# A staircase of single, paired and four-wide row tiles for gate/up, new due times, and down pieces in three steps

## The chip, the cores and the metric

The kernel runs on one core of one Trainium2 chip. The metric is device time in microseconds (us). TensorE is called PE below, VectorE DVE, ScalarE ACT, GpSimd POOL and SyncE SP; PSUM is the memory of eight banks into which PE writes, and from which DVE and ACT copy ("evict") to SBUF.

## What is computed

With `x` of 2048 rows and 640 columns, the output is `x + A(xn) + B(xn)`, where `xn` is the layernorm of `x`:

```python
def _A_ref(x, w_r, w_i):
    X = rfft2(x, axes=(-2, -1)) * (w_r + 1j * w_i)
    return irfft2(X, s=(S, D), axes=(-2, -1))

def _B_ref(x, w_gate, w_up, w_down):
    g = einsum("bsd,df->bsf", x, w_gate)
    u = einsum("bsd,df->bsf", x, w_up)
    return einsum("bsf,fd->bsd", g * u, w_down)

xn = _layernorm(x)
return x + _A_ref(xn, A_w_r, A_w_i) + _B_ref(xn, B_w_gate, B_w_up, B_w_down)
```

The weights `w_gate` and `w_up` are 640 x 1536, `w_down` is 1536 x 640, and `w_r`, `w_i` are 2048 x 321.

## The kernel before, in words

The rows are cut into 16 row tiles of 128, the 1536 hidden features into 12 blocks of 128, called features 0 to 11, and the 640 columns into five blocks of 128.

**Order.** No engine's order is written by hand. Each piece of work is a task with engines it may run on, an estimated duration, a priority (a lower number goes first) and what it reads and writes. `_Sched.plan` (line 155) lists them in advance: for each engine it takes the best priority, lets another task go first if that one ends within a slack (1500 ns for PE, 100 for names in `urgent`, line 1265, tile transposes `T0_0` to `T0_3` among them), and hands out PSUM banks. `caps` (lines 564 to 567) bound how many bank holdings a class may have at once: `glu` 4 (gate/up of 512 columns), `glu2` 2 (narrower gate/up), `acc` 5 (down), `a` 2 (pairs of banks for transposes and transforms). Each engine then runs its list in order, with semaphore waits.

**Stages.** (1) Loads of `x` (tiles 0 to 3 one by one, then 4 and 8 tiles) and of gate/up weights (features in groups 2, 2, 2, 2, 4) go out on SP; 10 warm-up rounds and small fill matmuls (lines 738 and 749) occupy PE meanwhile. (2) Layernorm by tile (groups of `_LN_GROUPS`; line 762): statistics on DVE (L785, L794) or ACT (L767, L776), then subtract and scale (L824, L831 or L830). Tiles 0 to 3 are transposed on PE (`T0`, L849) and copied to `XT`; later tiles by a transposing DMA (L837). (3) Forward transform over 8 groups of two tiles: butterflies S1 to S5 on DVE (L891 to L925), then a transform `R` on PE (L938) and its copy to `U`. (4) Gate/up (below). (5) When all of `U` is there, the spectral stage for 16 steps: D (L1055), C (L1078), multiplication by the filter on DVE (L1093, L1096), inverse IA (L1129, L1130), copy to `Z2`. (6) Inverse transform I on PE (L1158), by two tiles inverse butterflies V1 to V5 on DVE (L1182 to L1215). (7) Down: for each tile and half of the columns (the last tile in three pieces) 12 matmuls over the features into one bank (`ACC`, L1236), one more for the inverse transform (`IV`, L1248), the final addition of `x` on DVE (`FIN`, L1256), and a store.

**Gate/up.** For a group of row tiles ("chunk") and a feature, five matmuls for gate and five for up stream the chunk's columns of `XT`. `_CHUNKS` (line 508) holds tiles 0 and 1 alone, tiles 2-3 as a pair, and three chunks of four tiles. Chunks under four tiles take L997: one unit is two features, gate and up side by side in one bank for each (2 x 128 or 2 x 256 columns). Chunks of four take L977: one unit is one feature, gate and up in a bank of 512 columns each. ACT or DVE copies each bank to SBUF (L718 on ACT, L719 on DVE, helpers with many users), and DVE multiplies the two copies into `HT` (L1013 for four tiles, L1014 else). The units are sorted by the later of two due times, that of the rows (`c_at`) and that of the weights (`w_at`), and numbered for their priority (40 and up):

```python
w_at = [6.0 + opts.get("w_rate", 2.2) * opts.get("w_step", (0, 1, 2, 3, 4, 4))[ft // 2] for ft in range(12)]
c_at = [6.3 + opts.get("c_rate", 2.6) * (b0 + nb - 1) for b0, nb in _CHUNKS]
units = sorted((max(c_at[ci], w_at[ft | 1]), ci, ft) for ci in range(len(_CHUNKS))
               for ft in range(0, 12, 1 if _CHUNKS[ci][1] == 4 else 2))
```

**Down pieces.** Those of tiles 0 to 2 are three tasks of 5, 4 and 3 features (`cuts`, line 1229), the other 27 pieces one task of 12. The region of `w_down` for features 0 to 6 is taken by inverse tables until the spectral stage is over.

Of the kernel before, what the change touches and what calls it, by code (L numbers as in the profile page):

```python
# [504 lines left out]
_NW = 3  # L505
_WQ = 4
_GW_LOADS = ((0, 2), (2, 2), (4, 2), (6, 2), (8, 4))
_CHUNKS = ((0,1),(1,1),(2,2),(4,4),(8,4),(12,4))
_LP = 321
_YS = 1090  # L510
_NY = 3
# [39 lines left out]
def _build(nc, A_x, A_w_r, A_w_i, B_w_gate, B_w_up, B_w_down, out, opts=None):  # L551
    opts = opts or {}
    tabs = _build_tables()
    es = contextlib.ExitStack()
    with es:
# [7 lines left out]
        sch = _Sched()  # L563
        sch.caps = {"glu": opts.get("cap_glu", 4), "acc": opts.get("cap_acc", 5), "fill": 1}
        sch.caps["b"] = opts.get("cap_b", 3)
        sch.caps["glu2"] = opts.get("cap_glu2", 2)
        sch.caps["a"] = opts.get("cap_a", 2)
        lay = {}
        cur = [0]

        def alloc(name, size, at=None):
            if at is None:
                off = cur[0]
                cur[0] += size
            else:
                off = at
            lay[name] = (off, size)
            return sch.buf(name, off, size)
# [9 lines left out]
        b_x = alloc("X", 16 * 640, at=lay["Z2"][0])  # L588
# [166 lines left out]

        for gi, (b0, nb) in enumerate(_X_LOADS):
            dma("ld_x%d" % gi, v_x[:, b0:b0 + nb, :], xv[:, b0:b0 + nb, :], 128 * nb * (1800 if nb == 4 else 1400 if nb == 1 else 1280),
                [(b_x, ("s", b0, b0 + nb))], prio=(0.0, 0.003, 0.02, 0.03, 0.042, 0.06)[gi])
        muls = {}
        sd0 = None  # L760
        aset = set(opts.get("act_set", (1,))) | set(range(opts.get("act_stats", 6), 16))
        for gi, (b0, nb) in enumerate(_LN_GROUPS):
            pbase = 1.0 + 0.05 * gi if gi < 4 else opts.get("ln_prio", 6.1) + 0.05 * (gi - opts.get("ln_lead", 4))
            for b in range(b0, b0 + nb):
                if b in aset:
                    def em_sm(c, b=b):
# [53 lines left out]
            for b in range(b0, b0 + nb):  # L820
# [21 lines left out]
                def em_t0(c, b=b):  # L842
                    bk = bank_of(c.t)
                    ins = None
                    for j in range(5):
# [7 lines left out]
                       prio=pb, bank="pair" if b < opts.get("e0_split", 2) else "single", cls="a")  # L853
# [28 lines left out]
        for g in range(8):  # L882
            b = 2 * g
            gr = g % 2
            pf = opts.get("f_prio", 5.8) + 0.05 * g

            def em_s1(c, b=b, gr=gr):
                ins = None
# [64 lines left out]
        for i, (f0, nf) in enumerate(_GW_LOADS):  # L953
            for w_ in range(2):
# [1 line left out]
                    gvs[w_][:, :, f0 * 128:(f0 + nf) * 128], 5 * 128 * nf * (340 if nf == 2 else 280),  # L956
                    [(b_gw, ("s", w_ * _NGW + f0, w_ * _NGW + f0 + nf))], prio=(0.004, 0.012, 0.022, 0.032, 0.05)[i] + 0.001 * w_,
                    q="act" if w_ and i < 1 else "sp")
        w_at = [6.0 + opts.get("w_rate", 2.2) * opts.get("w_step", (0, 1, 2, 3, 4, 4))[ft // 2] for ft in range(12)]
        c_at = [6.3 + opts.get("c_rate", 2.6) * (b0 + nb - 1) for b0, nb in _CHUNKS]  # L960
        units = sorted((max(c_at[ci], w_at[ft | 1]), ci, ft) for ci in range(len(_CHUNKS))
                       for ft in range(0, 12, 1 if _CHUNKS[ci][1] == 4 else 2))
        for ui, (at_, ci, ft0) in enumerate(units):
            b0, nb = _CHUNKS[ci]
            n = 128 * nb
            rows = slice(b0 * 128, b0 * 128 + n)
            rr = ui % 3
            pu = 40.0 + 0.005 * ui
            pe_ = opts.get("eg_prio", 5.0) + 0.001 * ui
            ph_ = opts.get("h_prio", 5.0) + 0.001 * ui  # L970
            for u in range(2):
                ft = ft0 + u
                if nb == 4:
                    def em_gu4(c, ft=ft0, w=u, rows=rows):
                        bk = bank_of(c.t)
                        for j in range(5):
                            ins = c.e.matmul(ps[:, bk, :], v_gw[:, w, j, ft, :], v_xt[:, j, rows], start=(j == 0),  # L977
                                             stop=(j == 4))
                        return ins
                    gu = T("GU_%d_%d_%d" % (ft0, b0, u), "pe", 5.05 * _d_mm(n), em_gu4,  # L980
                           reads=[(b_gw, ("s", u * _NGW + ft0, u * _NGW + ft0 + 1)),
                                  (b_xta, ("s", b0 * 128, b0 * 128 + n)), (b_xtb, ("s", b0 * 128, b0 * 128 + n))],
                           prio=pu + 0.001 * u, bank="single", cls="glu")

                    def em_eg4(c, gu=gu, rr=rr, u=u):
                        return copy_on(c, v_gbf[:, rr, u, :], ps[:, bank_of(gu), :])
                    eg = T("eG_%d_%d" % (ui, u), ("act", "dve"), {"dve": _d_dve_psum(n), "act": _d_act(n)}, em_eg4,
                           writes=[(b_gbf, ("r", 2 * rr + u, 2 * rr + u + 1))], prio=pe_, frees=gu)
                    hold(gu, eg)
                    continue  # L990

                def em_gu(c, ft=ft, n=n, rows=rows):
                    bk = bank_of(c.t)
                    ins = None
                    for w in range(2):
                        for j in range(5):
                            ins = c.e.matmul(ps[:, bk, w * n:(w + 1) * n], v_gw[:, w, j, ft, :],  # L997
                                             v_xt[:, j, rows], start=(j == 0), stop=(j == 4))
                    return ins
                gu = T("GU_%d_%d" % (ft, b0), "pe", 10.15 * _d_mm(n), em_gu,  # L1000
                       reads=[(b_gw, ("s", w_ * _NGW + ft, w_ * _NGW + ft + 1)) for w_ in range(2)] + [
                           (b_xta, ("s", b0 * 128, b0 * 128 + n)), (b_xtb, ("s", b0 * 128, b0 * 128 + n))],
                       prio=pu + 0.001 * u, bank="single", cls="glu2")

                def em_eg(c, gu=gu, rr=rr, n=n, u=u):
                    return copy_on(c, v_gbf[:, rr, u, 0:2 * n], ps[:, bank_of(gu), 0:2 * n])
                eg = T("eG_%d_%d" % (ui, u), ("act", "dve"), {"dve": _d_dve_psum(2 * n), "act": _d_act(2 * n)}, em_eg,
                       writes=[(b_gbf, ("r", 2 * rr + u, 2 * rr + u + 1))], prio=pe_, frees=gu)
                hold(gu, eg)

            def em_h(c, ft0=ft0, rr=rr, n=n, rows=rows, nb=nb):
                if nb == 4:
                    return c.e.tensor_tensor(v_ht[:, ft0, rows], v_gbf[:, rr, 0, :], v_gbf[:, rr, 1, :], _OP.mult)  # L1013
                return c.e.tensor_tensor(v_ht[:, ft0:ft0 + 2, rows], v_gbf[:, rr, :, 0:n], v_gbf[:, rr, :, n:2 * n],  # L1014
                                         _OP.mult)
            T("H_%d" % ui, "dve", _d_dve_tt16(min(2 * n, 512)), em_h,
              reads=[(b_gbf, ("r", 2 * rr, 2 * rr + 2))],
              writes=[(b_ht, ("col", b0, b0 + nb))], prio=ph_)
# [6 lines left out]
        for t in range(16):  # L1025
# [4 lines left out]
            if t % (_WQ // 2) == 0:  # L1030
                q0 = 2 * t
                for w_ in range(2):
# [10 lines left out]
                    for i_, (dst, src_, nb_) in enumerate(parts):  # L1043
                        dma("ld_w%d_%d_%d" % (t, w_, i_), dst, src_, nb_,
                            [(b_wr[wr][0], ("r", b_wr[wr][1] + 8 * w_ + 2 * i_, b_wr[wr][1] + 8 * w_ + 2 * i_ + 2))],
                            prio=9.5 + 0.05 * t, semkey=("w", wr), after=[muls[opts.get("w_after", 15)]])

            eds = []
            for w in range(2):
                def em_d(c, t=t, w=w):  # L1050
                    bk = bank_of(c.t)
                    ins = None
                    for k in range(5):
# [5 lines left out]
                       prio=pq, bank="single", cls="b")  # L1059
# [12 lines left out]
            for g in range(2):  # L1072
# [4 lines left out]
                def em_c(c, q=q, g=g, ar=ar):  # L1077
# [3 lines left out]
                       prio=pg, bank="single", cls="b")  # L1081
# [37 lines left out]
                def em_ia(c, q=q, yr=yr, g=g):  # L1119
# [3 lines left out]
                    for k in range(5):  # L1123
# [10 lines left out]
                       prio=pg, bank="single", cls="b")  # L1134
# [12 lines left out]
        for a in range(16):  # L1147
            pa = 19.0 + opts.get("i_rate", 1.0) * a
            pc = 41.0 + 0.05 * a
            r2 = a % 2  # L1150

            def em_i(c, a=a):
# [3 lines left out]
                for k, (f, o) in enumerate(((0, 1), (1, 0), (1, 1), (0, 0), (2, 0))):  # L1156
# [4 lines left out]
                   prio=pa, bank="pair", cls="a")  # L1161
# [58 lines left out]
        for a in range(16):  # L1220
            pc = opts.get("acc_prio", 41.0) + 0.05 * a
            xs = a % 4
            dma("ld_xr%d" % a, v_xr[:, xs, :], xv[:, a, :], 128 * 1280, [(b_xr, ("r", xs, xs + 1))],
                prio=pc, semkey=("xr", xs))
            pieces = _LAST if a == 15 else ((0, 320), (320, 640))
            for hf, (c0, c1) in enumerate(pieces):
                rb = [("r", 640 * (a % 2) + c0, 640 * (a % 2) + c1)]
                sl3 = slice(c0, c1)
                cuts = (0, 5, 9, 12) if a < opts.get("acc_split", 3) else (0, 12)
                own = ag2 = None  # L1230
                for k0, k1 in zip(cuts[:-1], cuts[1:]):
                    def em_ag2(c, a=a, sl3=sl3, k0=k0, k1=k1, own=own):
                        bk = bank_of(c.t) if own is None else bank_of(own)
                        ins = None
                        for ft in _FT_ORDER[k0:k1]:
                            ins = c.e.matmul(ps[:, bk, 0:sl3.stop - sl3.start], v_ht[:, ft, a * 128:(a + 1) * 128],  # L1236
                                             v_wd[:, ft, sl3], start=(ft == _FT_ORDER[0]), stop=False)
                        return ins
                    kw = dict(bank="single", cls="acc") if own is None else dict(after=[ag2])
                    fts = _FT_ORDER[k0:k1]  # L1240
                    rd = [(b_wd, ("e", 640 * min(fts), 640 * (max(fts) + 1)))] if k1 - k0 < 12 else [(b_wd, None)]
                    ag2 = T("ACC_%d_%d_%d" % (a, hf, k0), "pe", (k1 - k0) * _d_mm(c1 - c0), em_ag2,
                            reads=[(b_ht, ("col", a, a + 1))] + rd,
                            prio=pc + 0.01 + 0.001 * hf + opts.get("acc0_prio", 0.0) * (a < opts.get("acc_split", 3)), **kw)
                    own = own or ag2

                def em_iv(c, own=own, a=a, sl3=sl3):
# [4 lines left out]
                       prio=opts.get("iv_prio", 5.0) + 0.05 * a + 0.01 + 0.001 * hf, after=[ag2])  # L1252

                def em_f1(c, own=own, a=a, xs=xs, sl3=sl3):
# [5 lines left out]
                       prio=opts.get("fin_prio", 41.0) + 0.05 * a - 0.001, frees=own, after=[iv])  # L1260
                dma("st_out%d_%d" % (a, hf), ov[:, a, sl3], v_out[:, a % 2, sl3], 128 * 2 * (c1 - c0), [],
                    prio=pc - 0.003, reads=[(b_out, rb[0])], semkey=("out", a % 2, hf))
# [86 lines left out]
```

## Time and profile before

| What | us |
|---|---|
| median of 6 runs (204.7 to 205.82) | 205.12 |
| the profiled execution's own time | 205.25 |
| its span, first to last instruction | 203.5 |
| first gate/up matmul starts (L997) | 7.64 |
| first four-wide gate/up matmul recorded (L977) | 37.41 |
| first D of the spectral stage (L1055) | 82.97 |
| first I (L1158) | 140.64 |

A page of the profile gives busy time by engine, the span in 40 slices (a digit is tenths of the slice), the chain of work that ended last, and groups of instructions by line. PEld is the loading of weights into PE. Matmuls are pipelined, and their ends are modelled. A line of a timeline holds start, length, engine, line, operation, tiles, shape and count of a run of like instructions. The clock of PE was full in all 40 slices. Seventeen of the 360 matmuls of L977 are missing from the records.

### The profile page before, as it was taken

The page shows a single profiled execution, that of the slowest core. Times are in us where ns is not written, and L with a number is a line of the kernel's source. Part 1 is how long each engine was busy: PE and PEld are TensorE (multiplying, and loading weights), DVE is VectorE, ACT ScalarE, POOL GpSimd, SP SyncE. Part 2 cuts the span into 40 slices and gives each one's busy share as a digit, 9 for nine tenths or more (in the row PEclk, how much of TensorE's full clock was granted, in tenths as well). Part 3 has the DMA queues.
Part 4 walks back from the last instruction along what each step waited for, and adds up shares of the span by engine and source line. Part 5 has one row for each costly group of instructions (what it writes and reads, how often), then busy time and mean ns, then how long its engine had stood idle before and what let it go on. Part 6 is the DMA issues. An engine that isn't in the chain of part 4 may idle for free.

```text
span 203.5 us, 5045 instructions
## 1 busy us (share of the span) xinstructions
PE 197.8 (97%) x1908; PEld 135.3 (67%) x1925; DVE 179.6 (88%) x513; ACT 129.6 (64%) x287; POOL 32.0 (16%) x108
## 2 busy tenths in 40 slices
PE   7999999999999999899999999999999999999995
PEld 7998899555454555456666666667777767777774
DVE  3589999999999997697988898864999999999983
ACT  3688999999977676869999999987611220200000
POOL 0000000000000000065744675463000000000000
PEclk9999999999999999999999999999999999999999
DMA  6999953030351897404354434004313332322322
GB/s 188 301 342 378 362 85 64 3 64 3 65 66 40 245 200 209 129 0 124 77 140 122 116 88 127 0 4 130 98 32 100 104 104 67 116 85 80 96 64 64
DMA packets 31543, 23.83 MB, mean 117 GB/s; under 512 B 10528, under 2 KB 29472, under 8 KB 31392
## 3 DMA queue, kind: packets, MB, share of 16 engines
q1 hardware_dynamic: 30720, 23.16, 42.2%
q10 hardware_dynamic: 800, 0.36, 0.6%
q8 instruction: 15, 0.25, 0.5%
q14 instruction: 8, 0.07, 0.1%
HBM read 18.92 MB, written 2.62 MB: 106 GB/s over the span
## 4 chain that ended last, share of the span: by engine, by line
PE 67%; DVE 20%; DMA 4%; SPq 4%; issue 2%; ACT 2%
PE ps L1236 26%; PE ps L977 24%; DMA arena<-in_A_x_dram 4%; SPq L712 4%; PE ps L997 3%; PE ps L1130 2%; PE ps L1129 2%; PE ps L1078 2%; PE ps L1158 2%; PE ps L1248 2%; DVE arena L1013 2%; PE ps L1055 2%; DVE arena L902 2%; DVE arena L891 2%; DVE arena L892 1%
## 5 line engine op out<-in xcount | busy, mean ns | idle before, releaser
L718 ACT ACTIVATE arena<-ps 128x512 bf16<-128x512 f32 (+6 forms) x214 | 106.0, 534 | 39.9 <-PE ps L1158 25.0
L977 PE MATMUL ps<-arena 128*128 128x512 bf16 x343 | 81.0, 379 | 1.0
L977 PEld LDWEIGHTS ps<-arena 128*128 128x128 bf16 x360 | 33.2, 98 | 35.6 <-ACT arena L718 2.1
L1236 PE MATMUL ps<-arena 128*128 128x320 bf16 (+2 forms) x396 | 55.8, 295 | 0.3 <-DVE arena L1256 0.3
L1236 PEld LDWEIGHTS ps<-arena 128*128 128x128 bf16 x396 | 37.6, 98 | 14.0 <-DVE arena L1256 0.6
L997 PE MATMUL ps<-arena 128*128 128x128 bf16 (+1 forms) x360 | 28.2, 237 | 0.0
L997 PEld LDWEIGHTS ps<-arena 128*128 128x128 bf16 x360 | 25.0, 98 | 2.2 <-ACT arena L718 0.5
L1093 DVE TENSOR_TENSOR arena<-ps,arena 128x256 bf16<-128x256 f32 x64 | 24.0, 417 | 0.1
L1106 POOL TENSOR_SCALAR arena<-arena 128x256 bf16<-128x256 bf16 x8 | 6.8, 855 | 89.8 <-DVE arena L1096 89.8
L1013 DVE TENSOR_TENSOR arena<-arena 128x512 bf16<-128x512 bf16 x36 | 15.1, 420 | 5.0 <-ACT arena L718 4.9
L719 DVE CAST arena<-ps 64x321 bf16<-64x321 f32 (+1 forms) x25 | 12.2, 490 | 6.3 <-PE ps L1130 5.9
L1256 DVE TENSOR_TENSOR arena<-ps,arena 128x320 bf16<-128x320 f32 (+2 forms) x33 | 15.5, 475 | 1.6 <-PE ps L1248 1.6
L1129 PEld LDWEIGHTS ps<-arena 128*128 128x128 bf16 x160 | 12.4, 114 | 2.8 <-ACT arena L718 0.4
L1129 PE MATMUL ps<-arena 128*128 128x64 bf16 x160 | 13.4, 196 | 0.0
L1130 PE MATMUL ps<-arena 128*128 128x64 bf16 x160 | 13.3, 197 | 0.0
L1130 PEld LDWEIGHTS ps<-arena 128*128 128x128 bf16 x160 | 11.2, 114 | 2.1
L1115 POOL TENSOR_SCALAR arena<-arena 128x65 bf16<-128x65 bf16 x32 | 12.0, 376 | 0.0
L1113 POOL COPY arena<-arena 128x63 bf16<-128x63 bf16 x32 | 8.5, 266 | 17.1 <-DVE arena L1096 17.0
L1096 DVE TENSOR_TENSOR arena<-ps,arena 128x130 bf16<-128x130 f32 x32 | 9.3, 292 | 0.0
L776 ACT ACTIVATE arena<-arena 128x640 bf16<-128x640 bf16 x11 | 9.1, 830 | 0.0
L1114 POOL COPY arena<-arena 128x63 bf16<-128x63 bf16 x32 | 8.9, 279 | 0.0
L891 DVE TENSOR_TENSOR arena<-arena 128x384 f32<-128x384 bf16 x16 | 8.8, 550 | 0.0
(63 smaller groups left out, 223.2 us busy)
## 6 DMA issues: line engine op xcount, KB each, us to landing
arena<-in_A_x_dram SPq DMA_DIRECT2D x20, 160.0 KB, 2.5
out_dram<-arena SPq DMA_DIRECT2D x31, 80.0 KB, 1.6
arena<-in_A_w_r_dram SPq DMA_DIRECT2D x8, 160.5 KB, 2.9
arena<-in_A_w_i_dram SPq DMA_DIRECT2D x8, 160.5 KB, 3.0
arena<-in_B_w_gate_dram SPq DMA_DIRECT2D x4, 320.0 KB, 5.8
arena<-in_A_x_dram SPq DMA_DIRECT2D x1, 1280.0 KB, 9.8
arena<-in_A_w_r_dram SPq DMA_DIRECT2D x14, 80.2 KB, 2.8
arena<-in_A_w_i_dram SPq DMA_DIRECT2D x14, 80.2 KB, 2.9
```

What stands on the lines that cost most here:

```text
L718: return c.e.activation(dst, src, _ACTF.Copy)
L719: return c.e.tensor_copy(dst, src)
L891: c.e.tensor_tensor(uo[:, o, :, 0:3, :], v_xb[:, b:b + 2, 0:6:2, :], v_xb[:, b:b + 2, 5:10:2, :], op)
L977: ins = c.e.matmul(ps[:, bk, :], v_gw[:, w, j, ft, :], v_xt[:, j, rows], start=(j == 0), stop=(j == 4))
L997: ins = c.e.matmul(ps[:, bk, w * n:(w + 1) * n], v_gw[:, w, j, ft, :], v_xt[:, j, rows], start=(j == 0), stop=(j == 4))
L1013: return c.e.tensor_tensor(v_ht[:, ft0, rows], v_gbf[:, rr, 0, :], v_gbf[:, rr, 1, :], _OP.mult)
L1093: c.e.tensor_tensor(dst, xh.unsqueeze(1).to_broadcast([128, 2, 32, 4]), wv, _OP.mult)
L1115: return c.e.tensor_scalar(yg[:, 128:193], yg[:, 256:321], -1.0, None, _OP.mult)
L1129: c.e.matmul(dst, l1, v_ti[:, q, 0, :], start=True, stop=False)
L1130: ins = c.e.matmul(dst, l2, v_ti[:, q, 1, :], start=False, stop=True)
L1236: ins = c.e.matmul(ps[:, bk, 0:sl3.stop - sl3.start], v_ht[:, ft, a * 128:(a + 1) * 128], v_wd[:, ft, sl3], start=(ft == _FT_ORDER[0]), st ...
L1256: return c.e.tensor_tensor(v_out[:, a % 2, sl3], ps[:, bk, 0:sl3.stop - sl3.start], v_xr[:, xs, sl3], _OP.add)
```

## The change

Tiles 0 and 1 are taken alone for features 0 to 3, as a pair for features 4 and 5; tiles 2-3 as a pair for features 0 to 5; all four together for features 6 to 11. The other chunks stay. With it go new due times, new priorities for layernorm (`ln_prio`, `ln_lead`) and forward butterflies (`f_prio`), a third pair of banks for class `a`, and three steps for all down pieces. The list that is used is the default of `chunks`; `_CHUNKS`, which holds other cuts (features 4 and 8), isn't read any more. The three `x..._prio` options keep their values.

```diff
-_CHUNKS = ((0,1),(1,1),(2,2),(4,4),(8,4),(12,4))
+_CHUNKS = ((0, 1, 0, 4), (1, 1, 0, 4), (0, 2, 4, 8), (2, 2, 0, 8), (0, 4, 8, 12), (4, 4, 0, 12), (8, 4, 0, 12), (12, 4, 0, 12))
...
-        sch.caps["a"] = opts.get("cap_a", 2)
+        sch.caps["a"] = opts.get("cap_a", 3)
...
-            pbase = 1.0 + 0.05 * gi if gi < 4 else opts.get("ln_prio", 6.1) + 0.05 * (gi - opts.get("ln_lead", 4))
+            pbase = 1.0 + 0.05 * gi if gi < 4 else opts.get("ln_prio", 5.9) + 0.05 * (gi - opts.get("ln_lead", 3))
...
-            pf = opts.get("f_prio", 5.8) + 0.05 * g
+            pf = opts.get("f_prio", 5.95) + 0.05 * g
...
-        w_at = [6.0 + opts.get("w_rate", 2.2) * opts.get("w_step", (0, 1, 2, 3, 4, 4))[ft // 2] for ft in range(12)]
-        c_at = [6.3 + opts.get("c_rate", 2.6) * (b0 + nb - 1) for b0, nb in _CHUNKS]
-        units = sorted((max(c_at[ci], w_at[ft | 1]), ci, ft) for ci in range(len(_CHUNKS))
-                       for ft in range(0, 12, 1 if _CHUNKS[ci][1] == 4 else 2))
+        w_at = [6.0 + opts.get("w_rate", 1.8) * opts.get("w_step", (0, 0, 2, 2, 4, 4))[ft // 2] for ft in range(12)]
+        chunks = opts.get("chunks", ((0, 1, 0, 4), (1, 1, 0, 4), (0, 2, 4, 6), (2, 2, 0, 6), (0, 4, 6, 12), (4, 4, 0, 12), (8, 4, 0, 12), (12, 4, 0, 12)))
+        c_at = [6.3 + opts.get("c_rate", 2.6) * (b0 + nb - 1) for b0, nb, _f0, _f1 in chunks]
+        units = sorted((max(c_at[ci], w_at[ft | 1]), ci, ft) for ci in range(len(chunks))
+                       for ft in range(chunks[ci][2], chunks[ci][3], 1 if chunks[ci][1] == 4 else 2))
         for ui, (at_, ci, ft0) in enumerate(units):
-            b0, nb = _CHUNKS[ci]
+            b0, nb = chunks[ci][:2]
...
-                cuts = (0, 5, 9, 12) if a < opts.get("acc_split", 3) else (0, 12)
+                cuts = (0, 5, 9, 12) if a < opts.get("acc_split", 16) else (0, 12)
```

More of the change, by code (lines that the diff above doesn't have):

```diff
@@ L757, in _build @@
             dma("ld_x%d" % gi, v_x[:, b0:b0 + nb, :], xv[:, b0:b0 + nb, :], 128 * nb * (1800 if nb == 4 else 1400 if nb == 1 else 1280),
-                [(b_x, ("s", b0, b0 + nb))], prio=(0.0, 0.003, 0.02, 0.03, 0.042, 0.06)[gi])
+                [(b_x, ("s", b0, b0 + nb))], prio=(0.0, opts.get("x1_prio", 0.003), opts.get("x2_prio", 0.02), opts.get("x3_prio", 0.03), 0.042, 0.06)[gi])
         muls = {}
@@ L1243, in _build @@
                             reads=[(b_ht, ("col", a, a + 1))] + rd,
-                            prio=pc + 0.01 + 0.001 * hf + opts.get("acc0_prio", 0.0) * (a < opts.get("acc_split", 3)), **kw)
+                            prio=pc + 0.01 + 0.001 * hf + opts.get("acc0_prio", 0.0) * (a < opts.get("acc_split", 16)), **kw)
                     own = own or ag2
```

## The prediction

> **What bounds the kernel now.** I read the page's busy rows and slices first, then the busy time by stage, then TensorE (PE) in order of time, then the chain that ended last.
>
> ```profile
> PE 197.8 (97%) x1908; PEld 135.3 (67%) x1925; DVE 179.6 (88%) x513; ACT 129.6 (64%) x287; POOL 32.0 (16%) x108
> ...
> PE   7999999999999999899999999999999999999995
> ...
> DVE  3589999999999997697988898864999999999983
> ACT  3688999999977676869999999987611220200000
> ...
> PEclk9999999999999999999999999999999999999999
> ```
>
> PE looks full throughout at full clock. Since busy matmuls hide gaps shorter than their pipeline, I count columns instead. In the chain below, ten 512-wide matmuls take 2.16 us (216 ns) and 24 of 320 take 3.26 us (135.8 ns): 0.4177 ns per column and 2.2 ns per matmul.
>
> ```profile
> 80.98 2.16 PE ps L977 x10
> ...
> 163.86 0.49 DVE arena L1256
> ...
> 174.38 3.26 PE ps L1236 x24
> ```
>
> The program needs 442,304 columns (gate/up 245,760, down 122,880, the rest transforms and transposes) in 1,836 matmuls after tile 0's transpose: 184.7 + 4.0 = 188.7 us. From the first gate/up matmul at 7.64 to the last at 201.05 are 193.4 us. All waits of PE together are thus some 4.7 us: PE's own work is the first bound.
>
> ```profile
> 7.64:14.80 7.16, 7.16 (x131) 6.98 (x128) 5.57 (x22) 5.06 (x15) 0.00 (x0) 1.00 1.13 326
> 14.80:22.69 7.89, 7.73 (x94) 6.47 (x91) 7.44 (x22) 7.08 (x19) 0.00 (x0) 1.00 1.07 380
> 22.69:37.41 14.72, 14.67 (x180) 13.52 (x182) 14.45 (x49) 14.38 (x37) 0.00 (x0) 1.00 0.48 116
> 37.41:66.00 28.59, 28.43 (x151) 13.38 (x154) 28.52 (x89) 25.54 (x55) 0.00 (x0) 1.00 0.24 41
> 66.00:82.97 16.97, 16.92 (x101) 8.60 (x101) 14.26 (x37) 11.62 (x20) 0.00 (x0) 1.00 0.82 207
> 82.97:138.50 55.53, 54.19 (x646) 33.88 (x657) 47.51 (x146) 51.04 (x118) 31.14 (x102) 1.00 0.34 87
> ...
> 141.68:201.40 59.72, 59.08 (x485) 43.72 (x483) 57.91 (x138) 9.23 (x15) 0.00 (x0) 1.00 0.29 87
> ```
>
> The columns after the length are PE, weight load, VectorE (DVE), ScalarE (ACT), GpSimd. There is a second bound close by: DVE is full from 22.69 to 66 (layernorm and the forward butterflies S1 to S5), and again from 141.68 to 201.40 (inverse butterflies V1 to V5 and the final adds), where 1.3 of its 1.8 idle us lie at the very end. Between them the spectral stage keeps ACT busy 51.0 of 55.5 us. A gain at the end thus needs PE's and DVE's chains both to move.
>
> **The change, part by part.** All sums are made against the profiled execution: span 203.5 us, own time 205.25 us, 0.13 above the median of 205.12.
>
> *The staircase on PE.* Gate/up of tiles 0 to 3 now takes 240 matmuls of 128 columns and 120 of 256; after it, 80 of 128 (two tiles, features 0 to 3), 80 of 256 (tiles 0-1 features 4, 5; tiles 2-3 features 0 to 5) and 60 of 512 (features 6 to 11). Columns stay 61,440; 140 matmuls go.
>
> ```profile
> 7.64 1.28 PE L997 MATMUL ps<-arena 128*128 128x128 bf16 x20
> 8.76 0.44 PE L849 MATMUL ps<-arena 128*128 128x128 bf16 x5
> 9.03 3.05 PE L997 MATMUL ps<-arena 128*128 128x128 bf16 x50
> 11.92 0.44 PE L849 MATMUL ps<-arena 128*128 128x128 bf16 x5
> 12.20 2.40 PE L997 MATMUL ps<-arena 128*128 128x128 bf16 x40
> 14.51 0.45 PE L849 MATMUL ps<-arena 128*128 128x128 bf16 x5
> 14.80 7.78 PE L997 MATMUL ps<-arena 128*128 128x128 bf16 x90
> ```
>
> From start to start, 50 single-tile matmuls take 11.92 - 9.03 = 2.89 us, 57.8 ns each; the same width in the R group of the chain takes 0.56 / 10 = 56.0. A 256-wide one is 109.2 by the line above. Before: 240 x 57.8 + 120 x 109.2 = 26.97 us. After: 80 x 57.8 + 80 x 109.2 + 60 x 216 = 26.32: -0.65 us. With 56.0 it is -0.36. I take -0.65, from the line's own rows. The Trainium skill (TensorE: Matmul & The Clock Gate, "Back-to-back issue gap") gives a sustained 81 ns for 128 columns and 131 for 512, weight loads included. By it, 160 singles fewer would bring another 160 x 23 = 3.7 us and the wide ones far more; the rows here (57.8 and 216) deny both, so the trace decides.
>
> *Work in hand before tile 3.* This is the part that can cost. Now the singles of tiles 0 and 1 hold 240 x 57.8 = 13.9 us of work while tiles 2 and 3 come; after, 80 x 57.8 + 20 x 109.2 = 6.8 us. Working it forward: features 0-1 of tile 0 from 7.64 to 8.76; tile 1's transpose to 9.03; 60 singles (3.47 us) and tile 2's transpose (0.28) to 12.78; the pair of tiles 0-1 (20 x 109.2) to 14.97; with tile 3's transpose 15.25. Weights for features 4, 5 land at 11.24, so they do not bind. Tile 3 is scaled at 14.07 (DVE L831 starts 13.68, 0.39); its transpose starts at 14.51 behind a matmul and its copy by ACT (128x640, 0.70 us) ends at 15.70. If the planner places the transpose between the two pair units, PE waits some 0.28 us from 13.88 and never again; if after them, tile 3 is there at 14.97 + 0.44 + 0.70 = 16.1 and PE waits 0.85. Queued behind is all of PE, and ACT's evictions wait for that. I take 0.3, because the planner holds T0_3 as urgent. The Trainium skill speaks against such thinning: the same page ("HAM oscillation") warns of idle gaps over about 3.4 us, after which the clock halves. By it, a gap that long would cost itself and, as an estimate, half of as long again (1.7 us) in slow matmuls; the longest one I find is 0.85 us, and the clock row never falls.
>
> *Eviction waits on PE.* From 7.64 to 37.41 (29.77 us, one 512 matmul unrecorded, 0.22): 26.97 + three transposes 0.84 + two R groups 1.12 = 28.93 leaves 0.6 us of waits. 512-wide units have four banks instead of two, so I leave 0.2 of them: with tile 3, 0.5 after against 0.6, -0.1. Ends: -0.6 (none left) to +0.6 (0.85 + 0.35).
>
> *ACT and DVE.* Evictions: 16 of 128x256 fewer (0.38 each), 8 of 128x512 more (0.60): -6.1 + 4.8 = -1.3 us of ACT. H products: 8 of 256 fewer (0.28), 4 of 512 more (0.42): -0.56 us of DVE. PE hides both today; what they bring is DVE's last butterfly group, which ends at 79.80, some 0.5 earlier, and with it the spectral stage at 82.97. This DVE gain is what lets the PE gain through.
>
> *Priorities.* Layernorm of tiles 4 on goes from behind the forward butterflies to just ahead. Its instructions and its 12 transposing DMAs are the same; SP has nothing between its loads (issued by 18) and those of the inverse tables (66), so they are moved past nothing; GpSimd is idle until 83. The four-tile units of tiles 4 to 7 need their transposes, landed at 33.4 and used after 37: 3.8 us of cover. Without it, each us late costs a us. The sum of DVE work before the spectral stage is the same, so I take 0; ends -0.5 to +1.0 (one group of butterflies, some 5.5 us by its rows, split differently around ACT's statistics).
>
> *Third pair of banks (cap_a 3) and down pieces in steps (tiles 3 to 15).* 396 + 33 matmuls stay; 54 more tasks are only further semaphore marks, and all 396 already run at 135.8 ns. I take 0. From below: the wait of 0.45 us (163.86, for a final add) may go; from above: it may multiply, see the rivals.
>
> Sum: -0.65 - 0.1 = -0.75 on PE, -0.56 on DVE plus its slack. 205.25 - 0.75 = 204.5, less 0.13: **204.4 us**.
>
> **The rivals.** 0.3% (0.6 us) is about what a measurement of this kernel can tell from no change.
>
> *B, tile 3 too late:* the planner puts the transpose behind the pairs. For it: tile 3's copy ends at 15.70 today, after the 15.25 at which work runs out. Against: scaling ends at 14.07, and fewer H products stand before it. PE: -0.65 + 0.6, or with 56.0 ns -0.36 + 0.2: 205.0.
>
> *C, slower: final adds late in the last stage.* With every down piece cut in three, the transforms I can slip between steps, partial sums keep their five banks longer, and the third pair of banks takes from the same eight. DVE gives butterflies precedence and has 0.5 us of slack until 197, so PE meets more waits like the one at 163.86 (0.45 each). It decides from four more on: 4 x 0.45 - 0.75 = +1.05: 206.2. For it: DVE 57.9 of 59.7; a later spectral stage feeds it. Against: one such wait in 33 adds today, with the pieces of tiles 0 to 2 already cut.
>
> *D, nothing visible:* the planner's list order swallows the gain in new small waits; it counts with B.
>
> **How the numbers follow.** A 0.47 (204.4; 203.1 to 204.5), B with D 0.27 (205.0; 204.5 to 205.7), C 0.26 (206.2; 205.7 to 207.5). From below: -0.65 - 0.6 - 0.45 - 0.5 would be 202.9. The range 203.1 to 206.4 leaves out little of A and the upper part of C. Faster is A, same B and D, slower C.
>
> **What would show it.** A: L997 with 160 matmuls, L977 with 420 (less the unrecorded); L1014 8 and L1013 42 times; no PE gap over 0.5 us near 15; the first D (L1055) before 82.9; the first I (L1158) about 0.7 earlier than 140.64. B: a PE gap of 0.6 us or more at 14 to 16. C: several waits of L1236 for DVE L1256. The prediction is wrong if D starts after 84, if gaps before 37 exceed 1.2 us, or if the last stage alone changes by over 0.6.

## The result and the profile after

The kernel after takes 204.6 us (median of 29 runs, 204.27 to 206.34) against 205.12 us: a ratio of 0.9976, 95% interval 0.9966 to 0.9985, or -0.5 us (-0.3 to -0.7). A second timing of the same kernel on another occasion gave 0.9969 (0.9956 to 0.9983). The forecast was 204.4.

The page of the kernel after, rows that answer to those shown of before:

```profile
PE 196.5 (97%) x1766; PEld 127.7 (63%) x1785; DVE 179.3 (88%) x511; ACT 127.4 (63%) x277; POOL 32.0 (16%) x108
...
PEclk9999999999999999999999999999999999999999
```

PE has 142 recorded matmuls fewer (140 by the program) and is as full as ever. ACT has lost 2.2 us of work, DVE 0.3. The busy time by stage, in the same windows as before:

```profile
7.64:14.80 7.16, 6.22 (x94) 5.44 (x91) 4.79 (x19) 4.35 (x13) 0.00 (x0) 1.00 1.13 325
14.80:22.69 7.89, 7.60 (x71) 6.51 (x72) 7.82 (x24) 7.09 (x17) 0.00 (x0) 1.00 1.06 377
22.69:37.41 14.72, 14.62 (x86) 7.42 (x86) 14.69 (x48) 13.86 (x32) 0.00 (x0) 1.00 0.55 119
```

In the first window PE is busy 6.22 of 7.16 us, where it was busy all 7.16. PE in order of time shows where:

```profile
8.96 3.09 PE L998 MATMUL ps<-arena 128*128 128x128 bf16 x50 [0.26 <-DMA arena<-in_B_w_up_dram]
12.02 0.45 PE L849 MATMUL ps<-arena 128*128 128x128 bf16 x5
12.31 1.81 PE L998 MATMUL ps<-arena 128*128 128x128 bf16 x20
15.09 0.45 PE L849 MATMUL ps<-arena 128*128 128x128 bf16 x5 [0.97 <-DVE arena L831]
15.38 8.00 PE L998 MATMUL ps<-arena 128*128 128x256 bf16 x70
```

The transpose of tile 3 (L849 at 15.09) stands between the two pair units (10 of the 20 matmuls at 12.31 are already 256 wide), as the prediction had it, but PE waits about 1.1 us for DVE's scaling of tile 3 (L831), which starts at 14.65 instead of 13.68: its load landed at 12.77 us, against 11.80 before. R and D follow a little earlier all the same: the first D, with which the spectral stage begins, at 82.72 instead of 82.97.

This one pair of executions doesn't show the gain, though. The first gate/up matmul starts at 7.14 us in it, and at 7.64 before, for a reason that is no part of the change. These lines show tile 0's transpose and the fill matmuls ahead of that start, before and then after:

```profile
5.54 0.69 PE L849 MATMUL ps<-arena 128*128 128x128 bf16 x5
6.03 1.77 PE L738 MATMUL ps<-arena 128*128 128x64 bf16 x44
```

```profile
5.50 0.44 PE L849 MATMUL ps<-arena 128*128 128x128 bf16 x5
5.78 1.45 PE L738 MATMUL ps<-arena 128*128 128x64 bf16 x44
```

From start to start, a matmul of the transpose takes 107 ns before and 55 after: PE still ran at half rate there before, and did so until about 6.7 us. (The clock rows of the pages print full clock from the start, because the trace holds no clock record ahead of that.) Where the start falls differs from execution to execution: with the old cuts it is also 7.20, 7.21 and 7.52 in later kernels (e2, e12, e9), with the new ones 7.13 to 7.37, and the half rate there is also in e3, e9 and e11. In this pair the start brings 0.50 us, the matmuls from it to D 0.40, and PE's longer waits behind it take back 0.65: D is 0.25 earlier.

The chain that ended last, two rows that answer to those of before:

```profile
80.73 2.16 PE ps L978 x10
...
163.57 0.41 DVE arena L1257
```

The rate of a matmul has not changed, and the only wait for a final add in the last stage is still one (0.34 us instead of 0.45).

What the end hangs on is seen best across all kernels of this study. From each trace: the 512-wide ("four-wide") gate/up matmuls in PE's order ahead of the first D, the time of that D, what follows from it to the end of PE's last matmul, PE's waits of over 0.05 us from the one ahead of the first gate/up matmul to D (taken from start to start; unrecorded matmuls left out), and the profiled execution's own time. The kernels e1 to e12 are described in the next section.

| Kernel | 512-wide ahead of D | first D | D to last matmul | waits ahead of D | own time |
|---|---|---|---|---|---|
| before | 195 | 82.97 | 118.07 | 1.35 | 205.25 |
| after | 255 | 82.72 | 118.02 | 2.09 | 204.82 |
| after, again | 255 | 82.95 | 118.02 | 2.33 | 205.05 |
| e1_stair_only | 255 | 83.38 | 118.06 | 2.58 | 205.66 |
| e2_no_stair | 205 | 84.94 | 117.71 | 1.67 | 207.57 |
| e3_acc3 | 255 | 82.57 | 118.04 | 1.60 | 204.83 |
| e4_old_prio | 255 | 83.18 | 118.01 | 2.41 | 205.28 |
| e6_x3_early | 255 | 82.50 | 118.03 | not summed | 204.61 |
| e7_cut8 | 235 | 82.56 | 118.01 | 1.79 | 204.66 |
| e8_after_x3_late | 245 | 84.34 | 119.95 | not summed | 208.40 |
| e9_before_x3_late | 195 | 85.42 | 118.07 | not summed | 207.69 |
| e10_x4_early | 265 | 84.86 | 117.71 | 1.87 | 207.23 |
| e11_x34_early | 255 | 82.37 | 118.02 | 1.44 | 204.47 |
| e12_steps_only | 195 | 83.35 | 118.03 | not summed | 205.46 |

With 165 four-wide matmuls left behind D (of 360, 400 or 420 in all), everything from D to PE's end takes 118.0 to 118.1 us in all ten kernels that have it so. The time is then the start of D plus 122.1 or 122.3 us. In none of the kernels does PE wait by over 0.05 us right ahead of the last R or of D, so D comes when PE is through with its own work and the waits before it.

### The profile page after: what moved, and what is told of

It reads as the page before. It is cut to its first block, busy times and chain, and to the rows that moved or that the text cites. A ratio compares the mean times of both kernels' runs of the same rounds, so it can differ in the third digit from the quotient of the medians.

```text
span 203.0 us, 4750 instructions
## 1 busy us (share of the span) xinstructions
PE 196.5 (97%) x1766; PEld 127.7 (63%) x1785; DVE 179.3 (88%) x511; ACT 127.4 (63%) x277; POOL 32.0 (16%) x108
## 4 chain that ended last, share of the span: by engine, by line
PE 85%; DVE 6%; DMA 3%; SPq 3%; issue 1%; ACT 1%
PE ps L978 43%; PE ps L1237 23%; PE ps L998 4%; DMA arena<-in_A_x_dram 3%; SPq L712 3%; PE ps L1131 2%; PE ps L1079 2%; PE ps L1130 2%; PE ps L938 2%; PE ps L1159 2%; PE ps L1249 2%; PE ps L1056 2%; DVE arena L719 1%; ACT arena L718 1%; DVE arena L1257 1%
## 5 line engine op out<-in xcount | busy, mean ns | idle before, releaser
L718 ACT ACTIVATE arena<-ps 128x512 bf16<-128x512 f32 (+7 forms) x206 | 105.0, 547 | 40.0 <-PE ps L1159 24.0
L978 PE MATMUL ps<-arena 128*128 128x512 bf16 x401 | 93.9, 379 | 1.1
L978 PEld LDWEIGHTS ps<-arena 128*128 128x128 bf16 x420 | 38.9, 98 | 41.9 <-ACT arena L718 1.3
L1237 PE MATMUL ps<-arena 128*128 128x320 bf16 (+2 forms) x396 | 56.5, 295 | 0.2 <-DVE arena L1257 0.2
L1237 PEld LDWEIGHTS ps<-arena 128*128 128x128 bf16 x396 | 37.6, 98 | 13.9 <-DVE arena L1257 0.5
L1014 DVE TENSOR_TENSOR arena<-arena 128x512 bf16<-128x512 bf16 x42 | 17.6, 420 | 4.7 <-ACT arena L718 4.7
L998 PE MATMUL ps<-arena 128*128 128x128 bf16 (+1 forms) x160 | 14.2, 246 | 0.3 <-DMA arena<-in_B_w_up_dram 0.3
L1130 PEld LDWEIGHTS ps<-arena 128*128 128x128 bf16 x160 | 12.4, 114 | 2.8 <-ACT arena L718 0.4
L998 PEld LDWEIGHTS ps<-arena 128*128 128x128 bf16 x160 | 12.1, 98 | 1.8 <-issue 0.4
L1131 PEld LDWEIGHTS ps<-arena 128*128 128x128 bf16 x160 | 11.2, 113 | 2.1
L776 ACT ACTIVATE arena<-arena 128x640 bf16<-128x640 bf16 x11 | 9.1, 826 | 0.0
```

Of the source, the lines that this page charges most:

```text
L718: return c.e.activation(dst, src, _ACTF.Copy)
L1130: c.e.matmul(dst, l1, v_ti[:, q, 0, :], start=True, stop=False)
L1131: ins = c.e.matmul(dst, l2, v_ti[:, q, 1, :], start=False, stop=True)
```

## The experiments

Theory S, from the prediction: the staircase carries the gain by fewer matmuls, less what PE waits for tile 3; the other parts cost nothing. Rival P: the other parts carry it, and the staircase only trades matmuls for waits. Ratios are to the kernel before, of runs on the same chip.

**Taking the change apart.** Kernel e1_stair_only, before with the new cuts and their due times alone (these small diffs are abridged to the values that change):

```diff
-_CHUNKS, w_rate 2.2, w_step (0, 1, 2, 3, 4, 4)
+chunks of the change, w_rate 1.8, w_step (0, 0, 2, 2, 4, 4)
```

> Only the staircase and its due times on the kernel before; priorities, banks and down pieces as before. Theory S (the staircase carries the gain through 140 fewer matmuls, -0.65 us, less what PE waits for tile 3): 204.6, ratio 0.997 to 0.998, 160 matmuls of the narrow line, one PE gap of 0.3 to 1.2 us ahead of tile 3's transpose. Theory P (the new priorities, the third pair of banks and the steps carry it, the staircase alone only trades matmuls for waits): 1.000, 205.1, and the same gap.

Measured: 205.56 us, 1.0023 (1.0014 to 1.0032). The staircase alone makes the kernel slower than either theory had it; D starts at 83.38. PE's waits ahead of D rise from 1.35 to 2.58 us, which is more than its fewer matmuls save: 0.38 us for tile 3, 0.84 for an eviction at 18.4, and 0.68 in four waits between 29 and 39 us that e4 below explains. Theory S falls as far as the staircase was to carry the gain by itself.

Kernel e2_no_stair, the kernel after with the cuts and due times of before:

```diff
-chunks of the change, w_rate 1.8, w_step (0, 0, 2, 2, 4, 4)
+((0, 1, 0, 12), (1, 1, 0, 12), (2, 2, 0, 12), (4, 4, 0, 12), (8, 4, 0, 12), (12, 4, 0, 12)), w_rate 2.2, w_step (0, 1, 2, 3, 4, 4)
```

> The kernel after with the old cuts of tiles 0 to 3 and the old due times; all other parts new. Theory S: 1.000, 205.1, no PE gap over 0.3 us before 22 us. Theory P: 0.997 to 0.998, 204.6.

Measured: 207.51 us, 1.0109 (1.0089 to 1.0128). Both theories miss: the other parts alone cost 2.2 us by the ratio, 2.4 by the medians. PE waits no more than before ahead of D (1.67 us), but the planner puts one more unit (10 matmuls, 2.16 us) ahead of D, and the last group of forward butterflies ends at 81.27 instead of 79.81. From D to PE's last matmul it takes only 0.36 us less, though PE has 2.16 us less to do there, and to the end of the span not less at all (120.55 against 120.49 us). PE waits there now for DVE (0.7 us for final adds instead of 0.3, 0.6 us for filter products): that stretch is bound by the other engines as much as by PE.

Kernel e4_old_prio, the kernel after with the old priorities of layernorm and butterflies:

```diff
-ln_prio 5.9, ln_lead 3, f_prio 5.95
+ln_prio 6.1, ln_lead 4, f_prio 5.8
```

> The kernel after with the old priorities of layernorm and forward butterflies. Theory S: 204.6 (within 0.15), first D at 82.7. Theory P: 205.1, with the first D at 83.0 or later, because the butterflies of the last tiles end later.

Measured: 205.31 us, 1.0011 (1.0001 to 1.0021), D at 83.18: as rival P has it, but not for P's reason: the last butterflies end at 79.51, earlier than in the kernel after (79.87). With the staircase in place, the priorities are worth some 0.7 us. The timeline of this kernel shows where PE loses it (start, length, engine; behind a bracket, what ended the wait):

```profile
29.50 0.60 ACT L718 ACTIVATE arena<-ps 128x512 bf16<-128x512 f32 x1
29.98 0.84 ACT L776 ACTIVATE arena<-arena 128x640 bf16<-128x640 bf16 x1
...
30.69 0.21 ACT L776 ACTIVATION_READ_ACCUMULATOR arena<-arena 128x1 f32 x1
30.79 0.60 ACT L718 ACTIVATE arena<-ps 128x512 bf16<-128x512 f32 x1
31.26 0.75 ACT L767 ACTIVATE arena<-arena 128x640 bf16<-128x640 bf16 x1
31.44 0.76 PEld L978 LDWEIGHTS ps<-arena 128*128 128x128 bf16 x5 [0.53 <-ACT arena L718]
```

ACT evicts one bank, makes one statistic of layernorm (L767 or L776), evicts the next: 1.2 to 1.3 us from eviction to eviction, while PE fills a bank in 5 x 216 = 1.08. After a few of these the four banks are full, and PE waits (0.13 to 0.20 us ahead of four matmuls that start between 29.0 and 38.8, 0.68 us in all; e1, with the old priorities too, has the same four). The same stretch of the kernel after:

```profile
29.60 0.59 ACT L718 ACTIVATE arena<-ps 128x512 bf16<-128x512 f32 x1
30.45 0.60 ACT L718 ACTIVATE arena<-ps 128x512 bf16<-128x512 f32 x1 [0.27 <-PE ps L978]
30.95 0.82 ACT L776 ACTIVATE arena<-arena 128x640 bf16<-128x640 bf16 x1
```

Here ACT waits for PE. No wait of a matmul start over 0.05 us is left between 24 and 40 us, nor in e3 below, which has the new priorities. e3 and e4 both have tile 3 in time, and D starts at 82.57 and 83.18. Two scalings on ACT (L830, 0.82 us each) that old priorities have are gone as well; DVE makes them.

Kernel e3_acc3, the kernel after with steps in the pieces of tiles 0 to 2 only (`acc_split` 16 back to 3):

> The kernel after with steps in the down pieces of tiles 0 to 2 only. Theory S: as the kernel after, 204.6 (within 0.15), the last stage from the first I to the end unchanged within 0.1 us. Theory P: 204.9 or more, with the wait of PE for a final add near 163.5 back at 0.45 us against 0.34.

Measured: 205.07 us, 0.9987 (0.9974 to 1.0). By the ratio (204.85 us) it lies between both; PE's wait for a final add is back at 0.44 us, as P has it. Its counterpart is e12_steps_only, the kernel before with `acc_split` 3 made 16 and nothing else:

> The kernel before with nothing new but three steps in all down pieces. Where all other parts are new, steps went with 0.2 us (ratio 0.9976 with, 0.9987 without), and where the old priorities stand as well (0.9987 of 1.0011 over 1.0023). Theory S (steps are only semaphore marks): 1.000, within 0.001, the first I to the end unchanged within 0.1 us. Theory P (steps let transforms start sooner, so that the last butterflies end sooner): 0.998 to 0.999, the last I (174.2) about 1.2 us earlier and the end 0.2 us.

Measured: 205.15 us, 0.9997 (0.9979 to 1.0015), which can't tell the two apart. The traces do: own time less the start of D is 122.26 to 122.28 us in before, e1, e3 and in a later kernel (e9) without steps, and 122.09 to 122.11 in all seven with steps and 165 matmuls behind D, e12 among them. Of these 0.17 us, 0.06 lie before the last final add; behind it, the last store's issue on SP takes 0.33 us instead of 0.43, when two others don't stand right ahead of it. So the steps bring 0.17 us at the very end.

Class `a` was not run by itself: planned with a bound of 2 instead of 3, the kernel after has the same tasks in the same order and the same banks on every engine, so this part of the change does nothing.

**Tile 3 and the work in hand.** In e8_after_x3_late the load of tile 3 goes behind the weights of features 6 and 7 (`x3_prio` 0.03 to 0.034), in e9_before_x3_late the same is done to the kernel before.

> The kernel after with the load of row tile 3 issued behind the weights of features 6 and 7, so that it lands some 2 us later. Theory S, cover lost: PE's gap ahead of the transpose grows by some 2 us to 3 us and the time by 1.5 to 2: 206.1 to 206.6. Rival H: under 0.5 us, 205.0.

> The kernel before with the same later load of row tile 3. Its single tiles hold 13.9 us of work instead of 6.8. Theory S, cover lost: no PE gap over 0.3 us at 14 to 18 us, 205.1 (within 0.3). Rival H says the same, since nothing is lost; a rise of over 1 us would mean that tile 3's lateness costs by another way (its butterflies on DVE), and then the later load of the kernel after is no measure of cover.

Measured: e8 209.65 us, 1.0214 (1.018 to 1.0248); e9 207.54, 1.0102 (1.0075 to 1.0128): both above all that was expected. Tile 3 lands at 13.8 and at 15.5 us. In e9 PE waits at the transpose in spite of all single tiles in hand:

```profile
12.09 4.37 PE L997 MATMUL ps<-arena 128*128 128x128 bf16 x70
17.84 0.45 PE L849 MATMUL ps<-arena 128*128 128x128 bf16 x5 [1.38 <-DVE arena L831]
18.12 4.67 PE L997 MATMUL ps<-arena 128*128 128x128 bf16 x50
```

Fifty singles stand behind the transpose in PE's order. They need no tile 3, but the list was made with a load that comes sooner. Then 1.8 us more are lost at 38.4, where the first four-wide unit (L977) waits for DVE (L912, a butterfly). So the work in hand counts only as far as the planner puts it ahead. And since e9 rises by 2.1 us, the later load costs in other ways too: as the expectation says, e8 is then no measure of the lost cover alone. In e8 the wait is longer. Its busy time in three stretches (columns as before; of the last three numbers the first is PE's granted clock):

```profile
14.00:17.00 3.00, 0.80 (x8) 0.47 (x5) 2.93 (x10) 1.15 (x4) 0.00 (x0) 1.00 1.05 357
17.00:18.50 1.50, 0.56 (x5) 0.30 (x5) 1.50 (x6) 1.47 (x4) 0.00 (x0) 0.70 1.17 366
18.50:21.00 2.50, 2.43 (x12) 1.71 (x13) 2.50 (x10) 2.00 (x7) 0.00 (x0) 0.50 1.05 419
```

PE stands for 2.58 us until 17.39. From about 17.6 to 21 us it runs at half clock (0.50), where a 256-wide matmul takes 0.213 us instead of 0.109, some 1.2 us in all; within that, from 17.95 to 18.57, PE waits once more for 0.62 us. The Trainium skill warns of idle gaps over some 3.4 us (TensorE: Matmul & The Clock Gate, "HAM oscillation"), from which the prediction argued; here a shorter gap was enough, so 3.4 us is not a safe distance. All six executions of e8 have a mean granted clock of 0.984 to 0.992, so it isn't the chance of one. DVE had tile 3 at 13.8 but scaled it only at 16.95: two forward butterflies (L901, L902; 1.3 us) stand between its statistics and its scaling in DVE's list, which they don't in e9. In the profiled executions (208.40 against 204.82 us) 1.6 us come before D, and 1.9 behind it, since 10 more four-wide matmuls are left there; e8's median lies 1.25 us above its profiled execution, which leaves that much of it unexplained.

Kernel e7_cut8 keeps more work ahead of tile 3, by the cuts of the unused constant (pairs to feature 8):

> The kernel after with the cuts of the unused constant: the pair of tiles 0-1 and that of tiles 2-3 reach feature 8, all four only from 8 on. 20 more matmuls (+0.05 us), but 9.0 us of work in hand before tile 3 instead of 6.8. Theory S, cover lost: gap ahead of the transpose gone, 203.8 to 204.2. Rival H: 204.5 to 204.8.

Kernel e6_x3_early loads tile 3 ahead of the weights of features 4 and 5 (`x3_prio` 0.0215):

> The kernel after with the load of row tile 3 issued ahead of the weights of features 4 and 5. If the wait for tile 3 is a loss that reaches the end (theory S, cover lost): the gap of 1.1 us ahead of the transpose falls under 0.3, those weights land 0.5 us later and still in time, and the time falls by 0.5 to 1.0 us against the kernel after: 203.6 to 204.1. If PE's early waits are made good later anyway (rival H: the butterflies on DVE set the spectral stage's start): gap gone, time 204.5 to 204.7.

Measured: e7 204.67 us, 0.9969 (0.9956 to 0.9982); e6 205.01, 0.998 (0.9968 to 0.9993). Neither is told apart from the kernel after by its ratio, as rival H has it. In e7 tile 3 landed at 11.9 and PE waited 0.38 us ahead of the transpose, then 0.51 at 17.8. In e6 the transpose of tile 3 waits no more (under 0.05 us), but that of tile 2 does, 0.35 us, since a statistic of tile 3 now stands ahead of tile 2's scaling on DVE: the wait has moved to the tile before. (PE also waits 0.45 us for up weights at 8.5 us, but so it does, 0.43 us, in the kernel after.)

**Was the 1.1 us chance, and what is the wait at 17.6?** after_again repeats the kernel after; e10_x4_early loads tiles 4 to 7 ahead of the weights of features 6 and 7 (their priority 0.042 to 0.031); e11_x34_early does that and what e6 does.

> The kernel after itself, for a second profile on the same chip as the two below. If the late landing of row tile 3 in its first profile (12.77 us, against 11.7 to 11.9 in the other kernels with the same loads) was chance: landing near 11.8, the wait ahead of its transpose 0.3 to 0.4 us instead of 1.1, and in its place a wait of 0.5 to 0.8 us near 17.6 for ACT. If it belongs to the kernel: 1.1 us again.

> The kernel after with the load of row tiles 4 to 7 issued ahead of the weights of features 6 and 7, which the staircase needs only from 22 us on. Theory Q (ACT stands at 17 us on the statistics of tile 6, whose load hasn't landed, with gate/up evictions queued behind it, and PE waits for those): those rows land near 14.8 us, ACT's wait and PE's wait of 0.5 to 0.8 us near 17.6 go, the first D comes 0.4 to 0.8 us earlier, and the time falls by as much against the kernel after: 203.8 to 204.2. Rival R (PE's early waits are made good before D, because the butterflies on DVE set its start): the wait goes, D and the time stay within 0.15 us.

> As the last one, and row tile 3 ahead of the weights of features 4 and 5. Theory Q: both waits small, 203.6 to 204.2, at least as fast as the last one. Rival R: as the kernel after within 0.2 us; moving tile 3 alone had brought nothing (ratio 0.998).

Measured: after_again 204.62 us, 0.9969 (0.9956 to 0.9983), and tile 3 landed at 13.0, so that the transpose waited even longer:

```profile
15.32 0.45 PE L849 MATMUL ps<-arena 128*128 128x128 bf16 x5 [1.44 <-DVE arena L831]
```

Of the ten profiled executions with these loads unchanged (tile 3 right behind the weights of features 4 and 5), seven have it landed at 11.7 to 12.0 us, and three at 12.8 to 13.0: both of the kernel after, and e12, which has the old cuts. So a late landing comes without the staircase too; whether two of two is chance isn't settled. Where tile 3 is in time, the other wait shows, here in e3_acc3, first ACT, then PE:

```profile
17.00 0.74 ACT L767 ACTIVATE arena<-arena 128x640 bf16<-128x640 bf16 x1 [0.69 <-DMA arena<-in_A_x_dram]
```

```profile
18.37 4.85 PE L998 MATMUL ps<-arena 128*128 128x256 bf16 x40 [0.51 <-ACT arena L718]
```

ACT stands 0.69 us on a statistic of tile 6, whose rows haven't landed, with the eviction that PE needs queued behind. Late tile 3 hides this wait, early tile 3 shows it, so the sum ahead of D changes by less than either.

e10 took 207.06 us, 1.0087 (1.0071 to 1.0103). Theory Q is not refuted by that: ACT's wait at 17 and PE's at 17.6 are gone (0.45 us at 15.7 instead); ACT now makes a statistic at 14.7 and the copy for tile 3 ahead of that eviction. But the planner, given other loads, put one more unit ahead of D (265 matmuls), the last butterflies ended at 81.19, and D started at 84.86: what e2 did. e11 has 255 again and the earliest D of all, 82.37, though ACT still waits 0.39 us for a load at 14.35 and PE 0.57 at 15.7; it took 204.53 us, 0.9968 (0.9956 to 0.998), the same as the kernel after beside it. No version here beats that by what can be measured.

## Why the prediction was right, and where it was not

The time, its sign and its size hold: -0.5 us measured, -0.7 forecast. The way there was partly wrong, and that the sum came out is in good part luck: the staircase with its waits was to bring -0.75 and brings +0.4 by itself (e1); priorities and steps were to bring nothing and bring -0.7 and some -0.2. The errors cancelled.

*Matmuls, -0.65.* The direction and the count hold (160 narrow ones, 420 wide, 8 and 42 H products as foretold). The size does not: PE's work ahead of D, at 0.4177 ns per column and 2.2 ns per matmul, falls by 140 x 2.2 = 0.31 us. The traces agree: from the first gate/up matmul to D, less the waits, are 74.0 us in before and e12, and 73.6 to 73.7 in the kernel after (both profiles), e1, e3, e4 and e11. The 57.8 ns of a single tile held a wait (0.08 us at 10.2); after, fifty of them take 12.02 - 8.96 = 3.06 us (61 ns), with 0.14 and 0.13 us of waits among them. The low end, -0.36, was the right one to take. That the rows deny the 81 and 131 ns of the Trainium skill (TensorE: Matmul & The Clock Gate, "Back-to-back issue gap") stands.

*Tile 3, +0.3.* Right where the load landed as before: 0.38 us in e1, e3, e4 and e7. In the two profiled executions of the kernel after it was 1.1 and 1.6 us, since the landing moved by 1.0 to 1.2 us; the prediction had taken a landing from one profile for fixed. Rival B's picture is thus half seen, without its result.

*Eviction waits, 0.2 left.* Under-sized when tile 3 is in time: 0.5 to 0.84 us near 17.6 in e1, e3, e4 and e7. The cause, ACT's statistic that waits for its load, is in the rows of before and was overlooked:

```profile
17.11 0.74 ACT L767 ACTIVATE arena<-arena 128x640 bf16<-128x640 bf16 x1 [0.40 <-DMA arena<-in_A_x_dram]
```

*DVE, D 0.5 us earlier.* Wrong as a cause: the last butterflies end at 79.87 and 80.12, against 79.81, so they give no earlier D. The last R follows them after 0.14 and 0.11 instead of 0.44 us: it stands in PE's queue, which is through sooner, in the first pair of profiles not least because it started 0.5 us sooner.

*Priorities, 0.* This step failed. With the staircase they are worth -0.7 us (e4), without it they came with +2.2 us or more (e2, steps included). The argument that the sum of DVE work stays the same left out that ACT alternates statistics with evictions, and that the planner's count of units ahead of D may change by one, which costs 2 us.

*Banks and steps, 0.* Right for the banks; the steps bring 0.17 us. Rival C did not come: one wait for a final add, 118.0 us behind D.

In order, from the timed medians: staircase alone +0.4, steps and banks on top -0.25, priorities on top -0.7. The first and the last are larger than their intervals; the -0.25 is not (1.0014 to 1.0032 against 1.0001 to 1.0021), and only the traces settle 0.17 of it. The explanation of e2 and e10 by one more unit rests on two kernels that agree (from the first gate/up matmul to D, less the waits, 76.2 and 75.8 us, 2.2 more than with the same cuts elsewhere), and was not tried by moving the unit alone. Which of the three values of the new priorities matters wasn't tried either.

## What to carry to other kernels

A part of a co-tuned change can't be valued by itself: the staircase was worth +0.4 us with the old priorities and about -2.7 with the new ones (e2 against the kernel after, by the ratios). Find the one event that all later work hangs on (here the first D; 118.0 us behind it in ten kernels), and cost each edit by what it does to the work and the waits ahead of that event, the planner's order among them. In a static order, work in hand is no cover unless it stands ahead of the instruction that waits. And one pair of profiles can differ by as much as the effect sought: here the start of gate/up scattered by 0.5 us, and a landing by over 1.

## What was not expected of the hardware

The landing of one load scatters: that of tile 3, with the same loads ahead of it, came at 11.7 to 12.0 us in seven profiles and at 12.8 to 13.0 in three; what delays it stays open. A stand of PE of 2.58 us was followed by half clock for some 3.4 us, and PE's rise to full rate at the start came at about 6.7 us in one profile and before 5.5 in another. And a store's issue on SP took 0.43 us right behind others, 0.33 alone.
